# Attention and slot 0 of a fused attention and expert kernel, written out as one list of pieces with named PSUM banks

## The chip, the cores and the metric

The kernel runs on one core of one Trainium2 chip. The metric is the device time of one execution in microseconds (us); the median of several executions is compared. TensorE is called PE here, VectorE DVE, ScalarE ACT, GpSimd POOL and SyncE SP, as in the profile.

## The reference

The kernel computes an attention over four batches of 768 tokens with eight heads of 64, whose output x (3072 tokens by 512) goes straight into a layer with eight experts, of which each token takes one. Of the attention, a token sees the neighbours closer than 16 positions, and one summary of each block of 32 tokens (the maximum of the block's keys, the mean of its values):

```python
k_sum = k.reshape(B, H, nb, block, D).max(axis=3)      # block 32, nb 24
v_sum = v.reshape(B, H, nb, block, D).mean(axis=3)
mask_l = np.abs(pos[:, None] - pos[None, :]) < window  # window 16
scores_s = scale * np.einsum('bhsd,bhnd->bhsn', q, k_sum) + np.log(block)
scores_all = np.concatenate([np.where(mask_l, scale * q @ k.T, -1e9), scores_s], axis=-1)
a = softmax(scores_all)
x = a @ np.concatenate([v, v_sum], axis=2)             # then to [3072, 512]
e_idx = np.argmax(x @ w_gate, axis=1)
...
    h = np.maximum(x[mask] @ w1[e], 0.0)               # 512 -> 1024
    ye = h @ w2[e]                                     # 1024 -> 512
    out[mask] = gate_w[mask, None] * eom[mask, e, None] * ye
```

## The kernel before, in words

The attention handles 24 tiles of 128 tokens, six to a batch; tile i is numbered by batch and place (tile 18 is the first of batch 3, and its buffers are called pr30, mn30 and so on). One tile passes these pieces. PE computes scores (L333) in two PSUM banks; DVE adds the mask (L338) and takes the smallest of each row and head, mn (L345, the scores are negated); POOL subtracts it (L350, pr<-pr,mn); ACT takes the exponential (L354); PE transposes the result (pt, L365) and ACT copies it out (L221); PE multiplies by the values (pv, L376); DVE divides by the sum (L386 to L390, into xs); the rows xs are stored to DRAM (x_dr, L395); PE transposes them (L402) and forms the router's logits (L411, L419), which DVE copies out (lg, L219).

For each batch there is preparation: the loads of k and q (raw_k, raw_q, L235, on SP's queue), a reordering copy (nat_k, nat_q, L246, most of them on POOL), transposes of them on PE (ktr, qtr, L291), copies into kt and qt on ACT (L221), the block maxima on DVE (km, L305), and their spread into kt on POOL (L312). The values are loaded into vw (L257, on SP, at the start also on POOL); their block means are summed on PE (ms, L264) and copied into each block of vw, every other copy on ACT (L221) and on DVE (L219, vw<-mst).

Once a batch has its logits, `route` finds each token's expert and its place in that expert's list: small operations on DVE (L435 to L479), counts on PE (rk, tot, L456 to L461), and one indirect DMA of POOL per tile that scatters the entries into the lists (l_dr, L484). After batches 0 and 1 a first table of slots of 256 tokens (`early_slots`, `slot_table_steps`, L699 to L765, on DVE) says which expert each slot belongs to. Slot 0 reads its list (lst, L866, POOL), gathers its rows of x (xg, L881, POOL), and PE transposes them (`take_plain`, xp, L1007) and starts with the experts' products (hp, L1017), among which the last attention pieces are placed by hand. From there on the expert slots follow one another.

All engines run in the order in which this program issues their instructions (a manual schedule). Before the change, that order comes from loops: for each tile i the loop issues scores(i + 2), values and norm of an older tile, turn_p(i), and so on, and work of other kinds is booked for a tile by `later(i, work)` in dictionaries (early, todo, put, scat, rts, end, small, mid, plan, pools). The tail from tile 21 on is written by hand. PSUM has eight banks under five tags (S, PT and PV two each, TR and MS one each). A piece takes its bank from a fixed cycle:

```python
    turn = [itertools.cycle(("TR", "S", "PT", "PV", "S", "PT", "PV"))]

    def bank(shape, name):
        tag = next(turn[0])
        return ps.tile(shape, F32, name=name, tag=tag, bufs=PB[tag])
```

A bank is free for a new piece when the operation that copies its last content out is done. `route` and the table yield a few times, so several of their small steps are issued in a row.

Of the kernel before, what the change touches and what calls it, by code (L numbers as in the profile page):

```python
# [39 lines left out]
EARLY_W = 2  # L40
# [16 lines left out]


# [143 lines left out]
def attention(tc, const, sa, sb, st, ps, dr, q, k, v, id_sb, c_sb, wg_sb, x_dr, l_dr, rt, moe, table, begin, swap):  # L202
# [56 lines left out]
    def means(b, m):  # L259
# [6 lines left out]
        if m == 2:  # L266
            nc.tensor.matmul(mp[96:P], lhsT=c_sb[0:W, C_AVG + 96:C_AVG + P], rhs=VW[b % 2][:, NB - 1, :, 0:D],
                             start=False, stop=True)
            evac(MT.rearrange("p h d -> p (h d)"), mp)

    def gather_means(b):
        mg = bank([P, H * D], f"mg{b}")
        nc.tensor.matmul(mg[LW:LW + 32], lhsT=c_sb[:, C_SUM:C_SUM + 32], rhs=MT.rearrange("p h d -> p (h d)"),
                         start=True, stop=True)
        ms[b] = sa.tile([P, H, D], F32, name=f"mst{b}", tag="mst", bufs=2) if b < B - 1 else \
# [3 lines left out]
    def put_means(b, tok):  # L279
        for blk in (2 * tok, 2 * tok + 1):  # L280
            evac(VW[b % 2][LW:LW + NS, blk, :, 0:D], ms[b][LW:LW + NS], engine="av"[blk % 2])

    ms, km, mps = {}, {}, {}

    def transposed(kind, b, u, g):
        n = nat[kind, b, u]
        pt = bank([P, 2, 256], f"{kind}tr{b}{u}{g}")
# [5 lines left out]
        return pt  # L293

    def prep_k(b, u, g):
        kt = KT[b % 2]
        pt = transposed("k", b, u, g)
        if b not in km:
            km[b] = sb.tile([P, HP, NS], F32, name=f"km{b}", tag="km", bufs=2)
        at = PAD + 4 * u * KW  # L300
        src = pt.rearrange("p x (i s) -> p x i s", s=64)
        dst = kt[:, 2 * g:2 * g + 2, at:at + 4 * KW].rearrange("p x (i w) -> p x i w", w=KW)
        evac(dst[:, :, :, 0:48], src[:, :, :, 0:48])
        evac(dst[:, :, :, 48 + NS:KW], src[:, :, :, 48:64])
        nc.vector.tensor_reduce(out=km[b][:, 2 * g:2 * g + 2, 8 * u:8 * u + 8],  # L305
                                in_=pt.rearrange("p x (n s) -> p x n s", s=32), axis=AX.X, op=ALU.max)
# [7 lines left out]
    def prep_q(b, u, g):  # L314
        qt = QT[(3 * b + u) % 2]
        evac(qt[:, 2 * g:2 * g + 2, :], transposed("q", b, u, g), -SCALE)
# [6 lines left out]
    def scores(i):  # L323
# [4 lines left out]
        for hp in range(HP):  # L328
            for y in range(2):
                blk = 2 * tok + y  # L330
                for x in range(2):
                    r = slice(64 * x, 64 * x + 64)
                    nc.tensor.matmul(sp[x][64 * y:64 * y + 64, hp, 0:W], lhsT=qt[r, hp, P * tt + 64 * y:P * tt + 64 * y + 64],  # L333
                                     rhs=kt[r, hp, blk * KW:blk * KW + W], start=True, stop=True)
        pr = sb.tile([P, 2, HP, W], F32, name=f"pr{b}{tok}", tag="pr", bufs=BUFS["pr"])
# [20 lines left out]
    def turn_p(i):  # L356
        b, tok = tiles[i]
        pr = prs.pop(i)
        e = i < HELD
        pTs[i] = (sa if e else sb).tile([W, 2, HP, P], F32, name=f"pT{b}{tok}", tag="pTe" if e else "pTl",  # L360
                                        bufs=BUFS["pTe" if e else "pTl"])
        for x in range(2):
            pt = bank([W, HP, P], f"pt{b}{tok}{x}")
            for hp in range(HP):
                nc.tensor.transpose(pt[:, hp, :], pr[:, x, hp, :], id_sb)  # L365
            evac(pTs[i][:, x], pt)

    def values(i):
        b, tok = tiles[i]
        pT = pTs.pop(i)  # L370
        pvs[i] = []
        for g in range(2):
            po = bank([P, 4, D + 1], f"pv{b}{tok}{g}")
            for h in range(4 * g, 4 * g + 4):
                for y in range(2):
                    nc.tensor.matmul(po[64 * y:64 * y + 64, h % 4, :], lhsT=pT[:, h % 2, h // 2, 64 * y:64 * y + 64],  # L376
                                     rhs=VW[b % 2][:, 2 * tok + y, h, 0:D + 1], start=True, stop=True)
            pvs[i].append(po)

    def norm(i):  # L380
# [3 lines left out]
        po = pvs.pop(i)  # L384
# [7 lines left out]
    def store_x(i):  # L392
        b, tok = tiles[i]
        n0 = b * S + tok * P
        (nc.sync if i >= 17 else nc.gpsimd).dma_start(x_dr[n0:n0 + P, :], xss[i].rearrange("p h d -> p (h d)"))  # L395
# [834 lines left out]
```

## Time and profile before

| what | value |
|---|---|
| median of three runs | 535.74 us (534.83 to 537.68) |
| the profiled execution, its own time | 536.84 us |
| its span | 535.0 us |
| mean granted clock of PE in it | 0.972 |
| PE busy | 491.0 us (92%) |
| DVE, ACT, POOL busy | 355.1, 313.1, 232.8 us |

The profiled execution is 1.10 us above the median of the three runs. Its time is the span and 1.84 us around it. The attention takes the first third of the span; the expert slots take the rest, and their matmuls make most of PE's busy time. PE's busy share is highest there, and lower in the attention.

### The profile page before, as it was taken

To read this page: it belongs to the slowest core of one execution; us is meant where nothing else is said; L and a number is where in the kernel's file an instruction comes from. 1 tells how busy PE (TensorE), PEld (TensorE's weight loads), DVE (VectorE), ACT (ScalarE), POOL (GpSimd) and SP (SyncE) were. 2 spreads that over 40 slices of the span, in tenths; PEclk is the share of its full clock that TensorE was granted. 3 is DMA by queue.
4 is the path that set the end of the run, shared out by engine and by line. 5 is a ranking of instruction groups with operands and counts; after the bars stand their busy time and mean duration, and the time that the engine had idled before them with its cause. 6 is when DMAs were issued, how large, how long until landed. Compare 5 with 4: busy or idle time off the path is not lost.

```text
span 535.0 us, 12519 instructions
## 1 busy us (share of the span) xinstructions
PE 491.0 (92%) x4348; PEld 405.3 (76%) x4348; DVE 355.1 (66%) x787; ACT 313.1 (59%) x612; POOL 232.8 (44%) x261
## 2 busy tenths in 40 slices
PE   7698999998987799999999999999999989989980
PEld 6556577486666686789898998989899869879870
DVE  3748479679876237797657667665756668668672
ACT  4475677576655545464646655554655567566581
POOL 8737535646684606736433240312224315214221
PEclk9899999998997799999999999999999999999996
DMA  9998957865329328996947748484673966967771
GB/s 235 199 236 199 278 129 179 197 154 128 82 56 324 117 92 266 242 168 193 328 141 254 254 168 312 126 310 150 245 260 137 310 212 216 319 210 228 264 238 29
DMA packets 106114, 109.53 MB, mean 205 GB/s; under 512 B 43150, under 2 KB 67886, under 8 KB 106032
## 3 DMA queue, kind: packets, MB, share of 16 engines
q1 hardware_dynamic: 97216, 90.04, 57.6%
q0 software_dynamic: 8816, 18.51, 11.4%
q8 instruction: 38, 0.62, 0.5%
q14 instruction: 44, 0.36, 0.3%
HBM read 98.33 MB, written 13.59 MB: 209 GB/s over the span
## 4 chain that ended last, share of the span: by engine, by line
PE 69%; ACT 9%; DMA 7%; issue 5%; POOL 4%; DVE 4%; SPq 1%; POOLq 0%; ACTq 0%; DVEq 0%
PE yp L1128 8%; PE yp L1127 8%; PE yp L1126 8%; PE hp L950 8%; PE hp L949 8%; PE hp L948 8%; PE pt L365 3%; PE hp L1017 3%; PE yp L1031 3%; PE pv L376 3%; PE sp L333 2%; ACT pr L354 2%; DMA raw<-in_moe_w_dram 2%; PE xp L930 2%; ACT pT L221 2%
## 5 line engine op out<-in xcount | busy, mean ns | idle before, releaser
L918 DVE TENSOR_TENSOR w2l<-raw,w2h 128x512 fp32r<-128x512 f32 x120 | 79.4, 685 | 40.3 <-ACT w2h L917 38.7
L917 ACT ACTIVATE w2h<-raw 128x512 fp32r<-128x512 f32 x120 | 72.9, 628 | 54.8 <-PE yp L1128 23.7
L950 PE MATMUL hp<-xhl,w1l 128*128 128x256 f32 x352 | 99.4, 283 | 0.0
L949 PE MATMUL hp<-xhl,w1h 128*128 128x256 f32 x352 | 99.4, 283 | 0.0
L948 PE MATMUL hp<-xhl,w1h 128*128 128x256 f32 x352 | 99.4, 284 | 0.0
L881 POOL DMA_INDIRECT xg<-x_dr,lst x34 | 39.3, 1155 | 118.1 <-PE xp L930 110.6
L918 DVE TENSOR_TENSOR w1l<-raw,w1h 128x512 fp32r<-128x512 f32 x117 | 74.5, 687 | 14.8 <-ACT w1h L917 13.5
L1126 PE MATMUL yp<-w2h,hh 128*128 128x512 f32 x200 | 80.1, 400 | 0.0
L1128 PE MATMUL yp<-w2h,hl 128*128 128x512 f32 x200 | 78.7, 394 | 0.1
L1127 PE MATMUL yp<-w2l,hh 128*128 128x512 f32 x200 | 78.6, 393 | 0.0
L917 ACT ACTIVATE w1h<-raw 128x512 fp32r<-128x512 f32 x120 | 67.0, 621 | 8.4 <-DMA raw<-in_moe_w_dram 6.9
L949 PEld LDWEIGHTS hp<-xhl,w1h 128*128 128x128 f32 x352 | 67.4, 191 | 1.1 <-issue 0.2
L948 PEld LDWEIGHTS hp<-xhl,w1h 128*128 128x128 f32 x352 | 67.2, 191 | 1.2 <-issue 0.2
L950 PEld LDWEIGHTS hp<-xhl,w1l 128*128 128x128 f32 x352 | 67.4, 192 | 0.0
L951 ACT ACTIVATE hh<-hp 128x256 fp32r<-128x256 f32 x88 | 33.4, 380 | 52.0 <-PE hp L950 50.4
L350 POOL TENSOR_TENSOR pr<-pr,mn 128x960 f32<-128x960 f32 x24 | 43.1, 1797 | 46.1 <-DVE mn L345 29.1
L952 DVE SCALAR_TENSOR_TENSOR hl<-hp,hh 128x256 fp32r<-128x256 f32 x88 | 35.9, 419 | 35.6 <-ACT hh L951 35.5
L1151 POOL DMA_INDIRECT out_dram<-y,lst x27 | 30.5, 1131 | 55.7 <-DVE y L1148 28.9
L221 ACT ACTIVATE pT<-pt 120x512 f32<-120x512 f32 x48 | 26.8, 596 | 41.2 <-PE pt L365 41.0
L338 DVE TENSOR_TENSOR pr<-sp,c_sb 128x480 f32<-128x480 f32 x48 | 29.2, 649 | 29.2 <-PE sp L333 29.2
L866 POOL DMA_INDIRECT lst<-l_dr,rowib x30 | 31.5, 1051 | 31.9 <-issue 21.8
L1128 PEld LDWEIGHTS yp<-w2h,hl 128*128 128x128 f32 x200 | 37.5, 188 | 8.6 <-DVE hl L1097 0.5
(206 smaller groups left out, 876.9 us busy)
## 6 DMA issues: line engine op xcount, KB each, us to landing
raw<-in_moe_w_dram SPq DMA_DIRECT2D x240, 256.0 KB, 5.2
raw_k<-in_k_dram SPq DMA_DIRECT2D x12, 512.0 KB, 6.0
raw_q<-in_q_dram SPq DMA_DIRECT2D x12, 512.0 KB, 6.2
vw<-in_v_dram SPq DMA_DIRECT2D x44, 128.0 KB, 4.9
x_dr<-xs POOLq DMA_DIRECT2D x17, 256.0 KB, 4.0
vw<-in_v_dram SPq DMA_DIRECT2D x33, 64.0 KB, 5.1
w1l<-in_moe_w_dram SPq DMA_DIRECT2D x8, 256.0 KB, 7.9
w2l<-in_moe_w_dram SPq DMA_DIRECT2D x8, 256.0 KB, 5.7
```

What stands on the lines that cost most here:

```text
L221: nc.scalar.activation(dst, src, AF.Copy, scale=1.0 if scale is None else scale)
L350: nc.gpsimd.tensor_tensor(pr, pr, mns.pop(i).unsqueeze(2).to_broadcast([P, H, W]), ALU.subtract)
L881: nc.gpsimd.indirect_dma_start(out=self.xg[t], out_offset=None, in_=self.x_dr[0:rows, :], in_offset=bass.IndirectOffsetOnAxis(ap=self.list ...
L917: nc.scalar.activation(hi, raw, AF.Copy)
L918: (lo_by or nc.vector).tensor_tensor(lo, raw, hi.bitcast(F32), ALU.subtract)
L948: nc.tensor.matmul(hp, lhsT=w_h[:, fs], rhs=self.xh[:, c, :], start=c == 0, stop=False)
L949: nc.tensor.matmul(hp, lhsT=w_h[:, fs], rhs=self.xl[:, c, :], start=False, stop=False)
L950: nc.tensor.matmul(hp, lhsT=w_l[:, fs], rhs=self.xh[:, c, :], start=False, stop=c == NC - 1)
L952: nc.vector.scalar_tensor_tensor(hl[:, j, :], hp, 0.0, hh[:, j, :].bitcast(F32), ALU.max, ALU.subtract)
L1126: nc.tensor.matmul(y, lhsT=hh[:, j, tk], rhs=w_h, start=j == 0, stop=False)
L1127: nc.tensor.matmul(y, lhsT=hh[:, j, tk], rhs=w_l, start=False, stop=False)
L1128: nc.tensor.matmul(y, lhsT=hl[:, j, tk], rhs=w_h, start=False, stop=j == NF - 1)
```

## The change

The loops, the dictionaries, the function `later` and the hand-written tail are gone. In their place stands a string of some 895 pieces, ORDER, and a table that says which function each name calls; a piece is its name, its numbers, and after a colon the letters of the PSUM banks that it takes (S, P for PT, V for PV, T for TR, M for MS). What used to be one step is split where it has parts on several engines: a transpose and the copy that empties its bank are separate pieces, and so are scores and mask. `route` (r.b, b the batch) and the first table (ta) now yield after each single operation, so that each is a piece. The engines of the copies of means are as before, but for one copy (block 31's, of tile 15) that moves from DVE to ACT. Before and after, the same operations run, the same number of them on PE. The table of the later slots, whose steps are single now too, is advanced three steps at a time (REST) and so is ready at the same place.

```diff
+REST = 3
+ORDER = """
+lk.0 lk.1 lk.2 lq.0 lq.1 lv.0.0.s lv.1.0.s cl.1 rk.0.v pk.0.0:T kk.0.0 cl.0 mk.0.0 pk.0.1:S kk.0.1 mk.0.1
+rk.1.a pk.1.0:P lv.0.1.p kk.1.0 pk.1.1:V kk.1.1 lv.1.1.p mk.1.0 mk.1.1 rk.2.p pk.2.0:T kk.2.0 pk.2.1:S lv.2.1.p kk.2.1 mk.2.0
...
-    turn = [itertools.cycle(("TR", "S", "PT", "PV", "S", "PT", "PV"))]
+    banks_of = []
...
-        tag = next(turn[0])
+        tag = {"S": "S", "P": "PT", "V": "PV", "T": "TR", "M": "MS"}[banks_of.pop(0)]
...
-    def prep_k(b, u, g):
-        kt = KT[b % 2]
-        pt = transposed("k", b, u, g)
...
+    def keep_k(b, u, g):
+        pt = banks["k", b, u, g]
...
+    def max_k(b, u, g):
...
-    for i, (b, tok) in enumerate(tiles[:n - AHEAD]):
...
-        scores(i + AHEAD)
-        for t in at[i]:
-            values(t)
-            norm(t)
...
+    for w in ORDER.split():
+        w, _, at = w.partition(":")
+        banks_of[:] = at
+        name, *args = w.split(".")
+        work[name](*(int(x) if x.isdigit() else x for x in args))
+    return [lambda: route_to(B - 1) for _ in range(TB)]
...
-            made = made or next(rest, None)
+            for _ in range(REST):
+                made = made or next(rest, None)
```

Three places show what the list moves. At the start, POOL's order around the reordering of the third part of batch 0's keys (nat_k02) was this before:

```order
L198 DMA l_dr_75<-fill_158 128x2
L215 MEMSET vw1_170 24x8x64
L246 COPY nat_k02_235<-raw_k02_182 128x1024
L257 DMA vw0_169<-in_v_dram 32x8x64 x11
L257 DMA vw0_169<-in_v_dram 16x8x64
L350 TENSOR_TENSOR pr00_317<-pr00_317,mn00_320 128x960
```

After the change it is this:

```order
L274 MEMSET vw0_169 24x8x64
L316 DMA vw0_169<-in_v_dram 32x8x64 x4
L305 COPY nat_k02_239<-raw_k02_176 128x1024
L316 DMA vw0_169<-in_v_dram 32x8x64 x5
L316 DMA vw0_169<-in_v_dram 16x8x64
L316 DMA vw0_169<-in_v_dram 32x8x64 x2
L422 TENSOR_TENSOR pr00_317<-pr00_317,mn00_320 128x960
```

Four of the twelve loads of values that POOL issues now stand ahead of that copy; the other eight stay behind it and ahead of the first subtraction (pr00).

On DVE, the steps just ahead of the smallest of tile 18 (mn30) were these before. inc1a, inc2a and inc4a belong to the first table, ssum, eo and pair to the routing of batch 1, pr31 is the mask of tile 19:

```order
L700 TENSOR_TENSOR inc2a_2194<-inc1a_2191 128x6
L699 COPY inc4a_2197<-inc2a_2194 128x4
L700 TENSOR_TENSOR inc4a_2197<-inc2a_2194 128x4
L472 TENSOR_REDUCE ssum1_2200<-ex1_2032 128x6
L473 TENSOR_SCALAR ssum1_2200<-ssum1_2200 128x6
L474 TENSOR_SCALAR eo1_2034<-eo1_2034 128x6
L475 RECIPROCAL ssum1_2200<-ssum1_2200 128x6
L476 RECIPROCAL eo1_2034<-eo1_2034 128x6
L478 TENSOR_TENSOR pair1_2206<-ssum1_2200,eo1_2034 128x6
L479 COPY pair1_2206<-tok_156 128x6
L345 TENSOR_REDUCE mn30_2209<-pr30_2137 128x8
L338 TENSOR_TENSOR pr31_2255<-sp310_2237,c_sb_68 128x480
```

After the change:

```order
L278 COPY vw0_169<-mst2_1674 24x8x64
L628 COPY inc1a_2187<-t_early_2048 128x1
L630 TENSOR_TENSOR inc1a_2187<-t_early_2048 128x7
L560 CAST posi1_2190<-pos1_2147 128x6
L563 TENSOR_REDUCE ssum1_2192<-ex1_2027 128x6
L565 TENSOR_SCALAR ssum1_2192<-ssum1_2192 128x6
L628 COPY inc2a_2195<-inc1a_2187 128x2
L630 TENSOR_TENSOR inc2a_2195<-inc1a_2187 128x6
L417 TENSOR_REDUCE mn30_2198<-pr30_2144 128x8
L567 TENSOR_SCALAR eo1_2029<-eo1_2029 128x6
L569 RECIPROCAL ssum1_2192<-ssum1_2192 128x6
L410 TENSOR_TENSOR pr31_2234<-sp310_2216,c_sb_68 128x480
```

Before, nine steps of the table (six of them stand above the rows shown) and seven of the routing lie between the copy of means into vw and mn30. Now seven steps lie there; the others have moved behind mn30, or ahead of the mask of tile 18.

On SP's queue, around the load of the first part of batch 3's queries (raw_q30), before, where vw0 is the buffer of batch 2's values:

```order
L235 DMA raw_k30_1400<-in_k_dram 128x8x128
L235 DMA raw_q30_1506<-in_q_dram 128x8x128
L257 DMA vw0_169<-in_v_dram 64x8x64
L257 DMA vw0_169<-in_v_dram 32x8x64
L257 DMA vw0_169<-in_v_dram 64x8x64
L257 DMA vw0_169<-in_v_dram 16x8x64
L235 DMA raw_k31_1518<-in_k_dram 128x8x128
```

After the change:

```order
L294 DMA raw_k30_1391<-in_k_dram 128x8x128
L316 DMA vw0_169<-in_v_dram 32x8x64 x2
L316 DMA vw0_169<-in_v_dram 64x8x64 x2
L316 DMA vw0_169<-in_v_dram 32x8x64
L316 DMA vw0_169<-in_v_dram 16x8x64
L316 DMA vw1_170<-in_v_dram 48x8x64
L316 DMA vw1_170<-in_v_dram 64x8x64
L294 DMA raw_k31_1510<-in_k_dram 128x8x128
L294 DMA raw_q30_1550<-in_q_dram 128x8x128
L294 DMA raw_k32_1627<-in_k_dram 128x8x128
```

The last loads of batch 2's values now stand ahead of the load of raw_q30 and not behind it.

Two more moves have no rows here. On PE, the values of tile 21 (16 matmuls) stand ahead of the transposes of slot 0's gathered rows (xp) and not behind them. And of the pieces that take a PSUM bank, 240 take one that an earlier piece of the list has used; counted in pieces of the list between the step that empties a bank and the piece that takes it next, the distance is six or less for 21 of them after the change (in three the emptying is written behind the taking), and for none before.

## Rows read from the trace of the kernel before

**Rows 1.** Windows by stage: busy us of each engine (and instructions), clock, DMA share.
```profile
64.00:119.00 55.00, 51.24 (x780) 37.14 (x778) 40.02 (x105) 38.56 (x75) 28.21 (x31) 1.00 0.70 173
119.00:143.00 24.00, 21.38 (x359) 16.15 (x358) 20.52 (x63) 15.07 (x32) 14.93 (x19) 0.93 0.52 111
143.00:178.70 35.70, 27.25 (x372) 19.29 (x370) 24.66 (x65) 19.44 (x33) 25.89 (x30) 0.88 0.59 186
178.70:430.00 251.30, 251.26 (x1645) 220.55 (x1646) 161.87 (x361) 140.81 (x285) 90.76 (x93) 0.99 0.67 214
```

**Rows 2.** Timeline of PE: start us, length us, work, [idle before it <- releaser].
```profile
24.36 1.09 PE L365 MATMUL pt<-id_sb,pr 128*120 128x128 f32 x8 [2.38 <-ACT pr L354]
...
25.38 1.06 PE L264 MATMUL ms<-vw,c_sb 64*32 64x512 f32 x8
...
48.95 1.54 PE L333 MATMUL sp<-kt,qt 64*64 64x120 f32 x32 [0.99 <-POOL kt L312]
...
74.12 1.25 PE L365 MATMUL pt<-id_sb,pr 128*120 128x128 f32 x8 [0.76 <-DVE km L305]
...
103.05 1.04 PE L264 MATMUL ms<-vw,c_sb 64*32 64x512 f32 x2 [1.11 <-DMA vw<-in_v_dram]
...
114.59 1.25 PE L365 MATMUL pt<-id_sb,pr 128*120 128x128 f32 x8 [0.76 <-DVE km L305]
...
128.61 0.18 PE L456 MATMUL rk<-ohb,tri 128*128 128x48 bf16 x1 [2.25 <-DVE km L305]
...
170.76 1.15 PE L376 MATMUL pv<-vw,pT 120*64 120x65 f32 x32
...
177.81 0.48 PE L1007 MATMUL xp<-id_sb,xg 128*128 128x128 f32 x1 [2.82 <-DMA xg<-x_dr,lst]
```

**Rows 3.** Timeline of SP's DMA queue: issues around the load of raw_q30.
```profile
95.76 0.39 SPq L235 DMA_DIRECT2D raw_q<-in_q_dram  x1
96.24 2.63 SPq L257 DMA_DIRECT2D vw<-in_v_dram  x4
```

**Rows 4.** Timeline of POOL: the start, then the road to the gather xg.
```profile
10.68 1.03 POOL L246 COPY nat_k<-raw_k 128x1024 f32<-128x1024 f32 x1
...
11.66 4.26 POOL L257 DMA_DIRECT2D vw<-in_v_dram  x7
...
138.54 1.04 POOL L246 COPY nat_q<-raw_q 128x1024 f32<-128x1024 f32 x1
...
143.36 1.78 POOL L350 TENSOR_TENSOR pr<-pr,mn 128x960 f32<-128x960 f32 x1 [3.78 <-DVE mn L345]
...
156.20 0.97 POOL L484 DMA_INDIRECT l_dr<-pair,posi  x1 [0.19 <-DVE mn L345]
...
158.18 1.80 POOL L350 TENSOR_TENSOR pr<-pr,mn 128x960 f32<-128x960 f32 x1
...
165.60 1.02 POOL L866 DMA_INDIRECT lst<-l_dr,rowia  x1 [5.62 <-DMA l_dr<-pair,posi]
```

**Rows 5.** Timeline of DVE: copies of means into vw, and mn30.
```profile
44.72 0.42 DVE L219 COPY vw<-mst 24x512 f32<-24x512 f32 x1
...
123.83 1.31 DVE L219 COPY vw<-mst 24x512 f32<-24x512 f32 x1
...
138.68 1.19 DVE L219 COPY vw<-mst 24x512 f32<-24x512 f32 x1
...
142.07 1.14 DVE L345 TENSOR_REDUCE mn<-pr 128x8 f32<-128x960 f32 x1
...
158.42 1.84 DVE L219 COPY vw<-mst 24x512 f32<-24x512 f32 x1
```

**Rows 6.** Windows behind three idle times of PE (columns as in rows 1).
```profile
24.40:28.00 3.60, 3.60 (x54) 2.43 (x55) 1.95 (x3) 1.98 (x3) 3.60 (x3) 1.00 0.94 148
129.20:132.60 3.40, 3.40 (x24) 2.25 (x24) 3.16 (x12) 1.85 (x3) 3.20 (x7) 0.50 0.93 219
177.40:184.20 6.80, 5.94 (x51) 5.20 (x52) 1.70 (x6) 3.75 (x8) 4.95 (x5) 0.53 0.07 23
```

More of the change, by code (lines that the diff above doesn't have):

```diff
@@ L59, in most @@
+"""
 def most(h):
@@ L383, in norm @@
         den = st.tile([P, H], F32, name=f"den{b}{tok}", tag="den", bufs=BUFS["den"])
-        po = pvs.pop(i)
+        po = [banks.pop(("pv", i, g)) for g in range(2)]
         for g in range(2):
@@ L452, in route @@
         nc.scalar.activation(ex, d, AF.Exp)
+        yield
         eo = tmp("eo", [P, TB])
         nc.scalar.activation(eo, o1, AF.Exp, scale=-1.0)
+        yield
         rk = bank([P, TB + 1, E], f"rk{b}")
@@ L488, in route @@
             rt["scatters"].append(i.ins)
-    steps = [(b, u) for b in range(B) for u in range(3)]
     routes = {}
@@ L517, in attention @@
-    for tok in range(2, TB):
-        load_vw(0, tok, (0,))
-    for g in range(2):
-        prep_q(*steps[0], g)
-    k_sum(0, "v")
-    for u in range(3):
-        load("k", 1, u)
-    n = len(tiles)
-    live, at, held = {}, {}, []
-    for i in range(n):
-        at[i] = []
-        for _ in range(2):
-            if i > HELD and held:
-                live[held[0]] = i
-                at[i].append(held.pop(0))
-        held.append(i)
-    live[n - 1] = n
-    early, todo, put, scat, rts, end, small, mid = {}, {}, {}, {}, {}, {}, {}, {}
@@ L538, in later @@
-    def later(i, work, when=todo):
-        when.setdefault(i, []).append(work)
-    for s in range(2, len(steps)):
-        later(2 * s - 3, lambda s=s: [prep_q(*steps[s], g) for g in range(2)])
-    for b in range(1, B):
-        for tok, gs in ({2: (0, 1), 3: (2, 3, 4, 5)} if b == 1 else {0: (0, 1), 1: (2, 3), 2: (4, 5)}).items():
-            for x in gs:
-                later(TB * (b - 1) + tok, lambda b=b, x=x: prep_k(b, x // 2, x % 2))
-    for b in range(B):
-        first = live[TB * b]
-        for m in range(3):
-            later(first - (3 if b == 0 else 4) + m, lambda b=b, m=m: means(b, m), early if b == 0 and m == 2 else todo)
-        later(first - 1 - (b > 0), lambda b=b: gather_means(b), end if b else early)
@@ L552, in attention @@
-    for t in range(n):
-        first = live[t - t % TB]
-        later(max(live[t] - 2, first - 1), lambda t=t: put_means(*tiles[t]), put)
-    for i in range(AHEAD):
-        scores(i)
-        smallest(i)
-        subtract(i)
-        if i == 0:
-            reorder("q", *steps[1], "a")
-            load("q", *steps[3])
-            for g in range(2):
-                prep_q(*steps[1], g)
-            exps(0)
-    for i in range(3):
-        later(live[2 * TB - 1] + 4 + i, table, small)
-    plan = {
-        live[2 * TB - 1] + 6: [begin],
-        n - AHEAD - 1: [moe.take_plain],
-    }
@@ L633, in attention @@
-    assert not small and not plan and not pools and not scat and not early and not end
-    b = B - 1
-    def first(j, *n):
-        moe.early_first(j)
-        for x in n:
-            moe.split(1, x)
-    t = n - AHEAD
-    values(t - 1)
-    norm(t - 1)
-    turn_p(t)
-    exps(t + 1)
-    for x in put.pop(t):
-        x()
-    for x in mid.pop(t, []) + rts.pop(t, []):
-        x()
-    assert not todo.pop(t, None) and not put and not todo and not rts and not mid
-    store_x(t - 1)
-    first(0, "v", "p")
@@ L1055, in full_with @@
             if not self.slots.get(EARLY):
-                made = made or next(rest)
+                for _ in range(REST):
+                    made = made or next(rest)
                 if made:
```

395 lines of the change are left out of this document (199 added, 196 removed).

## The prediction

> **What bounds the kernel now.** I read the windows by stage first. From 178.7 us on PE has no gap: it is busy for 251.26 of 251.30 us up to 430 [rows 1]. In the three attention stages ahead of that it stands idle for 3.76, 2.62 and 8.45 us, at a clock of 1.00, 0.93 and 0.88 [rows 1]. So the expert slots cost what they cost, and the end of the kernel follows from the moment at which PE can begin them without a gap. That moment is the landing of xg, slot 0's gathered rows, for which PE waits 2.82 us until 177.81 [rows 2]. A change that only orders attention, routing and first table can move the end by what it moves that landing, and by the PE work that it takes from behind it.
>
> Next I followed xg back on POOL. The list lst is issued at 165.60, after 5.62 us of waiting for the scatters into l_dr to land; the last scatter is issued at 156.20; and the work that leads to it begins with the subtraction at 143.36, which waited 3.78 us for mn30 [rows 4]. From there to the last scatter POOL stands still nowhere for more than 0.2 us: two subtractions, two stores of x, seven scatters. So two things set xg: when DVE delivers mn30 (tile 18), which hangs on PE's and DVE's progress up to there, and then a run of POOL and DMA work of about 34 us that the change leaves as long as it is.
>
> The progress up to mn30 is that of PE with its waits. Those that matter are listed in the timeline: 0.99 us for the spread of km into kt, twice 0.76 us for km (the bank to be taken was still read by DVE), 1.11 us for a load of vw, 2.25 us for km again [rows 2].
>
> **The change, place by place.** All terms are for the profiled execution of 536.84 us; it lies 1.10 us above the median of 535.74, and I carry the sum over to the median as it stands. Nothing is removed or added, so each term is a wait that goes or comes.
>
> *The start.* Four POOL loads of vw now stand ahead of the copy nat_k02, which before began at 10.68 without a wait [rows 4]. Seven such loads took 4.26 us, 0.61 each [rows 4], so nat_k02 comes 2.43 us later, and behind it the last keys, the maxima, the first queries and the first scores. On the other side PE waited 2.38 us for the first exponential at 24.36, and the first group of block means, 1.06 us, which stood behind that wait [rows 2], now stands ahead of it and fills it. The wait of 0.99 us at 48.95 goes as well, since values of tiles 2 and 3 stand ahead of those scores now. 2.43 - 1.06 - 0.99 is +0.4 us. Bounds: +2.4, if neither cover holds, and -2.0, if the load order hides the whole delay behind other waits.
>
> *64 to 119 us.* The two waits of 0.76 us on km end, because the transposes of P after them take banks that were emptied long before; the 1.11 us on vw ends, because those loads no longer stand behind the load of raw_q30. That load was issued at 95.76 and the four loads behind it from 96.24 on, over 2.63 us [rows 3]; it can only go when POOL has emptied the buffer of raw_q, and nothing of this holds the vw loads. Together -2.6 us. Bounds: -3.8, all that PE stands idle in this stage [rows 1], and 0, if another wait takes their place.
>
> *119 to 143 us.* A copy of means that takes 1.31 us on DVE at 123.83 [rows 5] goes to ACT. DVE is the engine that PE waits for here (2.25 us, [rows 2]). But the counts rk, which ended that wait, now stand behind the values of tile 14, and these in turn wait for the last km of that batch, so 1.15 us of PE work (a group of values at 170.76, [rows 2]) that was done ahead of the wait comes behind it. -1.31 + 1.15 is -0.2 us. Bounds: -1.3 and +1.2, one of the two without the other.
>
> *The steps ahead of mn30.* Between the copy of means, which ends at 138.68 + 1.19 = 139.87, and mn30 at 142.07 lay 16 small steps in 2.20 us [rows 5]; seven are left, so 9/16 of that goes, 1.24 us. The copy itself took 1.19 us where others take 0.42 [rows 5], and it ended 0.29 us after POOL's copy nat_q of 138.54 did [rows 4]. That POOL copy now stands ahead of a scatter rather than behind it, some 2 us earlier, and so the copy of means should again take 0.42: 0.77 us. Together -2.0 us. Bounds: -2.0 and 0, if PE's scores for tile 18 come late and DVE waits instead. The steps taken out cost DVE the same time elsewhere, in its idle time ahead of masks. Of the seven scatters three instead of four are now ahead of tile 19's subtraction; their number up to the last one stays.
>
> *The wait for xg.* The values of tile 21, 1.15 us at full clock [rows 2], move from behind the transposes of xg to ahead of them, into the 2.82 us of waiting. -1.15 us; bounds 0, if xg landed when PE had just come, and -2.3, at half clock.
>
> The sum is 0.4 - 2.6 - 0.2 - 2.0 - 1.15 = -5.55 us: 531.3 us for an execution like the profiled one, 530.2 us for the median. All bounds together would be +3.6 and -11.4 us.
>
> **The rivals.**
>
> *Banks that are taken too early: slower.* The reuse of a PSUM bank within six pieces of its emptying occurs 21 times now and never before, in tiles 3 to 7, 12 to 14 and 19 to 23 above all. A wait of PE on a bank that DVE has not emptied was 0.76 us [rows 2]. At that price eight such waits (6.1 us) eat the gain, and twelve make it 9.1 - 5.55 = +3.6 us, 539.3 us. For it: DVE and ACT run one behind the other on each tile, and a piece written two places behind an emptying waits for it in full. Against it: with two banks to a tag and scores two tiles ahead, part of them will be free in time.
>
> *Steps held beside POOL: no change.* The copy of means at 158.42 took 1.84 us instead of 0.42; POOL's subtraction ran from 158.18 to 159.98, and the copy ended 0.28 us after it [rows 4, 5]. So such an operation of DVE stands still while POOL's runs. The change puts a step of that kind right behind the smallest of tiles 11, 14, 17 and 19, where that tile's subtraction begins on POOL. At 1.42 us each that is 5.7 us, which eats the sum: 535.9 us. Against it: DVE often has the first word there, since it goes on at once. The Trainium skill (SBUF — State Buffer, section Who interferes with whom) says so in general: a DVE instruction with two SBUF inputs, or in a mode that uses both ports, and a GpSimd instruction that reads SBUF lock each other out for a whole instruction, and the one issued first wins. The trace agrees for the copies, 1.84 against 0.42 us; for the small steps no row here shows it.
>
> *The scatters' landing sets the end: only the last term is left.* The wait of 5.62 us ahead of lst [rows 4] falls where the weights of slot 0 are loaded. If these loads start earlier by as much as PE does, the scatters meet them earlier too and land when they landed before. Then xg stays, and only the values moved into the wait count: 535.74 - 1.15 = 534.6 us. For it: a scatter takes up to 9 us from issue to landing here (156.20 to 165.60); against it: the scatters are issued ahead of the weights' loads in both orders.
>
> *The clock comes back too: a larger gain.* After the waits of 2.25 and 2.82 us the granted clock is 0.50 for 3.40 us and 0.53 for 6.80 us, the lower of its two levels (1.2 of 2.4 GHz) [rows 6]. Half of 3.40 and 0.47 of 6.80 are 4.9 us. If the shorter waits leave the clock up, 530.2 - 4.9 = 525.3 us. Waits of up to 1.11 us left it at 1.00 [rows 1, 2]; after the 2.38 us at 24.36 it was 1.00 too [rows 2, 6], so the wait before does not settle it. The Trainium skill (TensorE: Matmul & The Clock Gate, part 1) has an idle engine drop to half and a busy one return; the trace agrees on the two levels. By that rule a filled wait is worth more than its length.
>
> **How the numbers follow.** The forecast has 0.44, its own range is 527.5 to 533 us. The clock rival has 0.16, the landing 0.16, the held steps 0.10, the banks 0.14. A measurement of this kernel can tell about 0.5%, 2.7 us, from no change. Faster by more: the forecast, the clock, and 0.06 of the landing and the held steps, in which part of the early terms survives; 0.66. Within: the rest of these two and 0.02 of the banks; 0.22. Slower: 0.12. The range from 524.5 to 537.0 us leaves out the banks beyond their deciding point and a fifth of the clock's cases.
>
> **What the changed profile would show.** nat_k02 should begin near 13.1 us and the first scores 2 us later than before; no wait on km between 64 and 119 us, none on vw at the last group of means; the copy of means ahead of mn30 at 0.42 us with seven steps behind it; the subtraction of tile 18 about 4.4 us earlier, near 139; lst near 161; xg about as much earlier, with a wait of some 1.7 us ahead of it; and a PE without gaps behind it. I am wrong if new waits of PE on DVE or ACT appear with short bank distances, if lst still goes at 165, or if PE gets gaps behind xg, because weights or lists for the later slots then come too late.

## The result, and the profile after

The changed kernel took 528.50 us (median of four, 526.94 to 529.75) against 536.31 us of the kernel before in the same comparison (median of four): ratio 0.9854, 95% interval 0.981 to 0.9897, faster. The forecast was 530.2 us in a range of 524.5 to 537.0. The profiled execution took 527.46 us, with a span of 525.4 us; the one before had 535.0 us, so the traces differ by 9.6 us. On the two chips of the experiments the same changed kernel measured 1.0056 and 1.0055 times the kernel before, so the gain did not come again; what stands behind this is part of the experiments. Some executions of every kernel fall into a slower state, and the medians in the experiments leave them out.

The windows of the stages after, for [rows 1] (the columns are the same; the last two windows are cut at the landing of xg, which came earlier):

```profile
core 0: us, PE busy (x) PEld busy (x) DVE busy (x) ACT busy (x) POOL busy (x), PEclk, DMA share, GB/s
64.00:119.00 55.00, 51.79 (x783) 36.94 (x781) 38.98 (x102) 39.98 (x77) 28.43 (x28) 0.97 0.82 180
119.00:143.00 24.00, 22.23 (x383) 17.27 (x377) 21.53 (x66) 17.05 (x35) 18.74 (x26) 1.00 0.52 122
143.00:174.00 31.00, 26.18 (x408) 17.96 (x405) 24.37 (x74) 20.99 (x35) 25.58 (x31) 1.00 0.59 200
174.00:430.00 256.00, 255.91 (x1652) 224.27 (x1653) 167.48 (x366) 145.75 (x294) 92.02 (x94) 1.00 0.65 217
```

From 64 to 119 us PE idles for 3.21 of 55.00 us where it was 3.76, at a clock of 0.97 where it was 1.00; it idles less behind that, and from 174 us on it is busy for 255.91 of 256.00 us. The clock is 1.00 in the two stages ahead of xg, where it was 0.93 and 0.88.

PE's timeline (start, duration, operation, and in brackets the wait ahead of it and what ended it), for [rows 2]:

```profile
14.02 1.97 PE L359 MATMUL ktr<-id_sb,nat_k 128*128 128x128 f32 x8 [2.72 <-POOL nat_k L305]
...
18.15 1.97 PE L359 MATMUL qtr<-id_sb,nat_q 128*128 128x128 f32 x8 [2.16 <-DVE nat_q L305]
...
27.36 1.09 PE L432 MATMUL pt<-id_sb,pr 128*120 128x128 f32 x8 [0.71 <-ACT pr L426]
...
31.25 1.09 PE L432 MATMUL pt<-id_sb,pr 128*120 128x128 f32 x8 [1.82 <-ACT pr L426]
...
44.85 0.69 PE L447 MATMUL pv<-vw,pT 120*64 120x65 f32 x16 [0.98 <-DVE km L373]
...
77.50 1.20 PE L447 MATMUL pv<-vw,pT 120*64 120x65 f32 x32 [1.73 <-DVE km L373]
...
172.59 0.33 PE L945 MATMUL xp<-id_sb,xg 128*128 128x128 f32 x1 [0.31 <-DMA xg<-x_dr,lst]
...
174.09 0.55 PE L945 MATMUL xp<-id_sb,xg 128*128 128x128 f32 x3 [1.17 <-DMA xg<-x_dr,lst]
...
176.18 1.89 PE L955 MATMUL hp<-xhl,w1l 128*128 128x256 f32 x8
```

POOL's timeline, for [rows 4]:

```profile
10.54 2.34 POOL L316 DMA_DIRECT2D vw<-in_v_dram  x4
...
12.93 1.03 POOL L305 COPY nat_k<-raw_k 128x1024 f32<-128x1024 f32 x1
...
24.48 1.79 POOL L422 TENSOR_TENSOR pr<-pr,mn 128x960 f32<-128x960 f32 x1 [3.87 <-DVE mn L417]
...
28.36 1.79 POOL L422 TENSOR_TENSOR pr<-pr,mn 128x960 f32<-128x960 f32 x1 [2.10 <-DVE mn L417]
...
141.96 1.79 POOL L422 TENSOR_TENSOR pr<-pr,mn 128x960 f32<-128x960 f32 x1 [2.21 <-DVE eo L567]
...
154.58 0.96 POOL L581 DMA_INDIRECT l_dr<-pair,posi  x1
...
156.97 1.79 POOL L422 TENSOR_TENSOR pr<-pr,mn 128x960 f32<-128x960 f32 x1 [1.42 <-DVE mn L417]
...
160.37 1.02 POOL L805 DMA_INDIRECT lst<-l_dr,rowia  x1 [0.63 <-issue]
...
166.36 1.03 POOL L820 DMA_INDIRECT xg<-x_dr,lst  x1 [0.95 <-DMA lst<-l_dr,rowia]
```

DVE's steps around mn30, for [rows 5]:

```profile
139.31 0.67 DVE L278 COPY vw<-mst 24x512 f32<-24x512 f32 x1
...
140.59 0.16 DVE L630 TENSOR_TENSOR inc2a<-inc1a 128x6 f32<-128x6 f32 x1
...
140.67 1.15 DVE L417 TENSOR_REDUCE mn<-pr 128x8 f32<-128x960 f32 x1
```

Three lines of the trace before that the table needs, from the timelines of POOL, of SP's queue (the first loads of slot 0's weights) and of PE (its first products), and the loads' line after the change:

```profile
23.70 1.79 POOL L350 TENSOR_TENSOR pr<-pr,mn 128x960 f32<-128x960 f32 x1 [0.43 <-DVE mn L345]
...
155.84 5.42 SPq L979 DMA_DIRECT2D w1l<-in_moe_w_dram  x8
...
184.32 1.97 PE L1017 MATMUL hp<-xhl,w1l 128*128 128x256 f32 x8
```

```profile
156.34 5.46 SPq L918 DMA_DIRECT2D w1l<-in_moe_w_dram  x8
```

The subtraction L350 (now L422) comes once per tile on POOL and dates each tile in both traces; the lines above and rows 4 give some of the starts. Read so, the 9.6 us come from the places in the table (after minus before, us). The last column is the same difference for a second pair of traces, of the runs again2 (the changed kernel) and control (the order before), both on one chip of the experiments; its 1.3 us are the difference of their spans, 538.1 and 539.4. Of the forecast for the start, the 0.99 us at 48.95 lie behind tile 1, so +1.4 and -3.6 stand in the first two rows.

| from | to | change there | forecast | second pair |
|---|---|---|---|---|
| start | subtraction of tile 1 (23.70, now 28.36) | +4.66 | +1.4 | +3.65 |
| there | subtraction of tile 15 (119.21, 123.83) | -0.04 | -3.6 | +0.17 |
| there | subtraction of tile 17 (134.90, 135.79) | -3.73 | -0.2 | -3.73 |
| there | subtraction of tile 18 (143.36, 141.96) | -2.29 | -2.0 | -2.29 |
| there | lst (165.60, 160.37) | -3.83 | 0 | +0.35 |
| there | end of the last wait for xg (178.74, 174.09) | +0.58 | 0 | -1.10 |
| there | first products of slot 0 (184.32, 176.18) | -3.49 | -1.15 | -2.46 |
| there | end of the span (535.0, 525.4) | -1.46 | 0 | +4.11 |

The total is right and most of the terms are not: the start loses three times what I gave it, the stage behind it gains nothing, and what carried the result are the stage up to tile 17, the landing of the scatters and the clock behind xg. Of these three the second pair shows the first and the last again, and not the landing.

### The profile page after: what moved, and what is told of

Read it like the earlier page. It is cut to its first block, busy times and chain, and to the rows that moved or that the text cites. A ratio compares the mean times of both kernels' runs of the same rounds, so it can differ in the third digit from the quotient of the medians.

```text
span 525.4 us, 12487 instructions
## 1 busy us (share of the span) xinstructions
PE 484.8 (92%) x4348; PEld 401.7 (76%) x4348; DVE 354.6 (67%) x786; ACT 314.3 (60%) x613; POOL 232.8 (44%) x261
## 4 chain that ended last, share of the span: by engine, by line
PE 74%; DVE 8%; ACT 4%; POOL 4%; issue 3%; DMA 3%; POOLq 0%; DVEq 0%; ACTq 0%
PE yp L1072 8%; PE yp L1070 8%; PE yp L1071 8%; PE hp L889 8%; PE hp L888 8%; PE hp L887 8%; PE hp L955 3%; PE yp L969 3%; PE pv L447 3%; PE sp L400 2%; PE pt L432 2%; PE xp L869 2%; DMA raw<-in_moe_w_dram 2%; DVE pr L410 2%; PE qtr L359 2%
## 5 line engine op out<-in xcount | busy, mean ns | idle before, releaser
L820 POOL DMA_INDIRECT xg<-x_dr,lst x34 | 40.7, 1197 | 111.8 <-PE xp L869 99.6
L422 POOL TENSOR_TENSOR pr<-pr,mn 128x960 f32<-128x960 f32 x24 | 43.2, 1800 | 44.1 <-DVE mn L417 29.5
L1070 PEld LDWEIGHTS yp<-w2h,hh 128*128 128x128 f32 x200 | 37.7, 188 | 7.4
```

The source lines that it names most:

```text
L422: nc.gpsimd.tensor_tensor(pr, pr, mns.pop(i).unsqueeze(2).to_broadcast([P, H, W]), ALU.subtract)
L820: nc.gpsimd.indirect_dma_start(out=self.xg[t], out_offset=None, in_=self.x_dr[0:rows, :], in_offset=bass.IndirectOffsetOnAxis(ap=self.list ...
L1070: nc.tensor.matmul(y, lhsT=hh[:, j, tk], rhs=w_h, start=j == 0, stop=False)
```

## The experiments

Each time stands beside a ratio to the kernel before on the same chip; the runs went out in three groups of four, each on one chip. The ratio isn't the quotient of the two medians, so a difference between two kernels of a group comes out a little otherwise by ratios than by medians; where that matters both are given. The hybrids are cut from the two lists, the order before being written in the notation of the change with the banks that its cycle gave.

**The start as before, the rest changed (start54).** The first 54 pieces, up to the subtraction of tile 0, are those of the order before.

```diff
-rk.1.a pk.1.0:P lv.0.1.p kk.1.0 pk.1.1:V kk.1.1 lv.1.1.p mk.1.0 mk.1.1 rk.2.p pk.2.0:T kk.2.0
+rk.1.a pk.1.0:P kk.1.0 mk.1.0 pk.1.1:V kk.1.1 mk.1.1 rk.2.p pk.2.0:S kk.2.0 mk.2.0
...
-sc.0:SP ma.0 mi.0 su.0
+lv.0.1.p lv.1.1.p lv.2.1.p lv.3.1.p lv.4.1.p lv.5.1.p
...
+sc.0:SP ma.0 mi.0 su.0
```

> The changed list, but its first 54 pieces (up to the subtraction of tile 0) stand in the order of before: the copy nat_k02 ahead of all loads of values on POOL, the bank letters of before with it. Theory A (the new start costs some 4.5 us, which is carried on to the end because nothing ahead of xg absorbs it): the first subtraction near 21.5 us instead of 24.5, the subtraction of tile 13 some 3 to 4.5 us earlier than in the changed kernel, the time 524 to 525.5 us, a ratio to before near 0.979. Theory B (the delay is absorbed: POOL's scatters and the loads of weights set when xg lands): as the changed kernel, 528 us, ratio near 0.985.

Measured: 538.6 us, ratio 0.9980 (0.9950 to 1.0010). Its first subtraction is at 21.39 us, tile 13's at 102.62. The earlier start came, as theory A had it, and the time of theory A didn't.

**Order before up to tile 13, changed behind it (late13), and the reverse (early13).** Both are joined at the subtraction of tile 13.

```diff
 late13: pieces before, lk.0 ... su.13 | the changed list's other pieces in its order
 early13: changed pieces, lk.0 ... su.13 | the other pieces in the order before
```

> The order of before up to the subtraction of tile 13 (427 pieces), the changed order from there on. Theory A (all of the gain arises behind tile 13, and the start is a loss): faster than the changed kernel by the 4.4 us that its tile 13 lies behind, 524 us, ratio 0.978. Theory B (start and middle do not matter, the end of attention sets xg): 528 us, ratio 0.985. If the middle (64 to 119 us) gained as the prediction says, it is slower than the changed kernel by 2 to 3 us: 531 us, ratio 0.990.

> The changed order up to the subtraction of tile 13, the order of before from there on. Theory A: slower than before by the 4.4 us: 540 us, ratio 1.008. Theory B: as before, ratio 1.000. If the middle gained as the prediction says: faster than before by 2 to 3 us, ratio 0.995.

Measured: late13 539.3 us, 0.9987 (0.9955 to 1.0019), with tile 13 at 103.99; early13 544.17 us, 1.0072 (1.0041 to 1.0104), with tile 13 at 108.49, lst at 168.99 and the last transposes of xg at 183.47. The changed order up to tile 13 alone is slower, by 4.5 us at that tile.

**Changed up to tile 20, the tail as before (tail20).**

```diff
 changed pieces, lk.0 ... su.20 | the other pieces in the order before
```

> The changed order up to the subtraction of tile 20 (684 pieces), the order of before from there on; the values of tile 21 stand behind the transposes of xg again. Theory A (the scatters land 4 to 5 us earlier since none of POOL's copies stands ahead of them, and that is in the part kept): lst still near 160.5 us, xg near 172 to 174, the values again behind xg for 1.15 us and the clock low behind a wait of about 2.5 us, 3 us more: 531 to 533 us, ratio 0.992. Theory B (the gain is made behind tile 20, by what PE does in the wait for xg): 535 to 536 us, ratio 0.999.

Measured: 538.0 us, 0.9994 (0.9960 to 1.0028), profiled span 533.1 us. Its lst goes out at 160.83, near the 160.5 of theory A, and the ratio is that of theory B; what decides lies behind slot 0, as the run control shows further down.

None of the four stood where the first comparison would put it, so the next four, on another chip, began with the changed kernel itself.

**The changed kernel unaltered (again), and the start as before once more beside it (start54b).** No edit; and that of start54.

> The changed kernel unaltered, so that the edits beside it are compared on one chip. Theory A and theory B both: ratio to before 0.985, as in its own measurement. If the chip of the first four experiments is what made them slow (each of them had stretches behind 200 us in which PE, ACT and DVE all waited for nothing that the profile shows), the ratio here tells how much of the gain such a chip leaves: 0.985 on a chip like the first one, 0.99 to 1.00 on one like the second.

> The kernel start54 again, beside the changed kernel on one chip. Theory B (the delay of the start is absorbed between tile 18 and xg): the same time as the changed kernel within 1.5 us, first transposes of xg within 1 us of it. Theory A (the delay is carried to the end): 4 us faster.

Measured: again 542.51 us, 1.0056 (1.0028 to 1.0084); start54b 537.19 us, 1.0003 (0.9964 to 1.0042). So the start before makes the changed list faster on one chip, by 5.3 us by the medians and 2.9 by the ratios. In the traces the first subtraction comes 2.7 us earlier (21.62 instead of 24.34), tile 13's 6.2, and the last transposes of xg 6.3 (172.69 instead of 178.98): nothing up to xg takes a late start up. Some 1.2 us of that may be the one trace of again, since again2, the same list, has these transposes at 177.74.

The trace of again shows a part of why the ratio is not that of the first comparison. Behind slot 0 PE gets single instructions with pauses for which no semaphore is the cause ("issue"), though it had no gap there in both first traces:

```profile
223.39 0.28 PE L884 MATMUL hp<-xhl,w1h 128*128 128x256 f32 x1 [1.04 <-issue]
...
224.81 0.37 PE L885 MATMUL hp<-xhl,w1h 128*128 128x256 f32 x1 [1.14 <-issue]
...
227.64 0.37 PE L884 MATMUL hp<-xhl,w1h 128*128 128x256 f32 x1 [1.53 <-issue]
...
230.44 0.37 PE L886 MATMUL hp<-xhl,w1l 128*128 128x256 f32 x1 [1.73 <-issue]
```

**The last scatter of batch 1 later (scat).**

```diff
-... r.1 ... mi.20 su.20
+... mi.20 su.20 r.1
```

> The changed list with one piece moved: the last scatter of batch 1 stands behind the subtraction of tile 20 on POOL, so that it is issued near 158.8 us instead of 154.6, behind the start of the loads of slot 0's weights (156.3) instead of ahead of it. Theory C (the scatters land late when they meet those loads; in the kernel before the last one was issued 0.4 us behind their start and lst waited until 9.4 us after its issue, in the changed kernel it left 1.8 us ahead of them and lst did not wait): lst at 166 to 168 us, xg some 6 us later, the time 3.5 to 5 us above the changed kernel. Rival (the landing takes its 5 us anyway): lst at 164, the time 1.5 to 2.5 us above it.

Measured: 546.55 us, 1.0142 (1.0098 to 1.0186), 4.0 us above again (4.6 by the ratios). POOL's timeline:

```profile
162.19 0.98 POOL L578 DMA_INDIRECT l_dr<-pair,posi  x1
...
168.90 1.00 POOL L802 DMA_INDIRECT lst<-l_dr,rowia  x1 [4.67 <-DMA l_dr<-pair,posi]
```

The scatter goes out 5.7 us later than in again (156.53 there) and not at 158.8 as expected, since POOL stood 4.67 us for the smallest of tile 20 before the subtraction that is now ahead of it. lst goes out 5.7 us later too (163.16 there). From the scatter to lst it is 6.7 us here, all of it landing, and 6.6 in again, where POOL did the subtraction and a copy meanwhile. So the later issue accounts for the whole shift, and the run does not show that the scatter lands more slowly behind the loads of weights: neither theory was put to the test as it stood.

**The values of tile 21 behind xg (va21).**

```diff
-va.21.0:P va.21.1:P ... tk.0 ... tk.1
+tk.0 ... tk.1 va.21.0:P va.21.1:P
```

> The changed list with the values of tile 21 behind the transposes of xg, as before. Theory of the prediction: 1.15 us of PE come back behind xg, 1 to 2 us above the changed kernel. Theory D (the wait for xg, 1.15 us longer then, makes PE fall to the lower clock behind it, as in the kernel before): 4 to 5 us above it, a granted clock near 0.5 for some us behind xg.

Measured: 544.9 us, 1.0121 (1.0079 to 1.0163), 2.4 us above again. In its trace PE waits 1.49 us for xg at 177.67, where again waits 0.35. The size (3.5 us by the ratios) agrees roughly with 1.15 us of values and as much of new waiting, but the granted clock stayed at 1.00 in both from 165 to 190 us, so this run says nothing of the clock.

The last four, on the chip of the first group, were to price the start and to find what the starved stretch belongs to.

**The changed kernel unaltered, on that chip (again2).** No edit.

> The changed kernel unaltered, as the reference for the other three on this chip. If PE runs without a gap from the first xp to 250 us, as in the first profile, the ratio to the kernel before should be near 0.985; if PE has the stretch behind slot 0 (from about 222 us) in which it gets an instruction only every 0.7 us or more, near 1.000 to 1.006, as on the chip of the second comparison.

Measured: 541.33 us, 1.0055 (1.0025 to 1.0085), with the stretch.

**Only nat_k02 ahead of the loads (nat2).**

```diff
-rk.1.a pk.1.0:P lv.0.1.p kk.1.0 pk.1.1:V kk.1.1 lv.1.1.p mk.1.0 mk.1.1 rk.2.p pk.2.0:T
+rk.1.a pk.1.0:P rk.2.p lv.0.1.p kk.1.0 pk.1.1:V kk.1.1 lv.1.1.p mk.1.0 mk.1.1 pk.2.0:T
```

> The copy nat_k02 alone goes ahead of the four loads of vw; all else is the changed list. Theory L (the four loads are the price of the start): the copy begins 2.4 us earlier, near 10.5 us, the first subtraction comes at least 2 us earlier (22.4 or before instead of 24.5), tile 13's subtraction 2.5 to 4.5 us earlier, and the end comes 2 to 4.5 us earlier than that of the unaltered list. Rival (the order of the first queries and scores, or the half clock between 14 and 24 us, sets the start): the first subtraction gains under 1 us, and so does the end.

Measured: 540.02 us, 1.0032 (0.9997 to 1.0067), 1.3 us below again2 and within its interval. POOL's timeline:

```profile
10.82 1.03 POOL L302 COPY nat_k<-raw_k 128x1024 f32<-128x1024 f32 x1 [0.21 <-PE ktr L356]
...
21.43 1.80 POOL L419 TENSOR_TENSOR pr<-pr,mn 128x960 f32<-128x960 f32 x1
...
24.69 1.79 POOL L419 TENSOR_TENSOR pr<-pr,mn 128x960 f32<-128x960 f32 x1 [1.46 <-DVE mn L414]
...
29.42 1.04 POOL L302 COPY nat_q<-raw_q 128x1024 f32<-128x1024 f32 x1 [2.94 <-DMA raw_q<-in_q_dram]
...
30.42 1.79 POOL L419 TENSOR_TENSOR pr<-pr,mn 128x960 f32<-128x960 f32 x1
```

The first two subtractions come 2.9 us earlier than in again2 (24.33 and 27.54), as theory L had it, and the third doesn't (30.42, there 30.27): the next copy of queries now waits 2.94 us for its load. That load is the third of raw_q on SP's queue; eight loads of vw stand ahead of it where the order before has four, and it goes out at 19.18 us instead of 15.12. Tile 13 gains 0.93 us, less than two traces of the unaltered list differ there (107.43 and 108.68). Neither theory holds as it stood: the four loads on POOL are one price of the start, and behind it stands a second, the load of queries that comes behind more values on SP.

**The scatters spread out (thin).**

```diff
+    r["pad"] = const.tile([P, 256], F32, name="pad")
...
             nc.gpsimd.memset(rt["gap"][:, g:g + 1], 0.0)
+            if b >= 2:
+                for _ in range(3):
+                    nc.gpsimd.memset(rt["pad"], 0.0)
```

> The changed list with three small writes of POOL (256 columns each, about 0.3 us each by the rows of such writes) ahead of each scatter of batches 2 and 3, so that these twelve go out at about 2.2 us each rather than 1.27. Theory S (the run of scatters is what starves PE behind slot 0): PE's idle time between 210 and 250 us falls from some 7 us to under 3, and the end comes 4 to 9 us earlier than that of the unaltered list. Rival W (the weights' loads and PE's own place in its instructions do it): still 5 us idle or more, the end within 2 us, or later, since lst of the later slot waits for scatters that come up to 11 us later. Where the unaltered list has no such stretch on this chip, the run tells nothing but the price of later scatters.

Measured: 537.96 us, 0.9972 (0.9937 to 1.0006), 3.4 us below again2 by the medians and 4.5 by the ratios. Windows of 5 us (busy us of each engine, granted clock, DMA share, GB/s) of again2:

```profile
core 0: us, PE busy (x) PEld busy (x) DVE busy (x) ACT busy (x) POOL busy (x), PEclk, DMA share, GB/s
210.00:215.00 5.00, 5.00 (x14) 2.19 (x12) 3.67 (x13) 1.63 (x4) 4.11 (x8) 1.00 1.03 367
215.00:220.00 5.00, 5.00 (x43) 4.94 (x42) 1.56 (x3) 1.07 (x2) 4.01 (x7) 1.00 0.93 276
220.00:225.00 5.00, 1.65 (x10) 1.25 (x8) 1.53 (x10) 0.00 (x0) 4.24 (x9) 0.86 0.87 259
225.00:230.00 5.00, 1.75 (x6) 1.36 (x5) 0.00 (x0) 0.00 (x0) 2.91 (x5) 0.50 0.14 41
230.00:235.00 5.00, 4.65 (x25) 4.36 (x25) 3.60 (x23) 2.86 (x8) 0.00 (x0) 0.62 0.00 0
235.00:240.00 5.00, 5.00 (x33) 4.51 (x32) 4.83 (x17) 3.94 (x9) 0.00 (x0) 1.00 0.21 56
```

And of thin:

```profile
core 0: us, PE busy (x) PEld busy (x) DVE busy (x) ACT busy (x) POOL busy (x), PEclk, DMA share, GB/s
210.00:215.00 5.00, 5.00 (x23) 3.09 (x22) 3.64 (x10) 0.84 (x2) 4.45 (x11) 1.00 0.86 279
215.00:220.00 5.00, 5.00 (x44) 5.00 (x44) 4.08 (x20) 1.80 (x5) 4.46 (x13) 1.00 1.04 342
220.00:225.00 5.00, 5.00 (x44) 5.00 (x43) 4.62 (x25) 2.06 (x5) 4.06 (x9) 1.00 0.51 153
225.00:230.00 5.00, 5.00 (x24) 4.12 (x23) 4.86 (x17) 3.65 (x8) 4.40 (x12) 1.00 0.57 109
230.00:235.00 5.00, 5.00 (x28) 4.14 (x27) 5.00 (x10) 4.04 (x8) 4.57 (x7) 1.00 0.22 15
250.00:255.00 5.00, 4.03 (x20) 3.07 (x19) 2.83 (x5) 3.01 (x7) 3.84 (x4) 1.00 0.74 245
255.00:260.00 5.00, 0.72 (x3) 0.73 (x4) 1.09 (x3) 0.98 (x2) 3.22 (x4) 0.66 0.82 292
```

PE's 6.95 us of idle time between 210 and 250 us, and the half clock behind them, are gone. In their place the later slot's rows come late: the last scatter goes out at 240.61 us, and PE waits for xg:

```profile
259.28 0.66 PE L870 MATMUL xp<-id_sb,xg 128*128 128x128 f32 x2 [5.26 <-remote]
```

These 5.26 us of new idle time stand against the 6.95 that went, and the end gains 3.4 or 4.5 us, at the edge of the 4 that I had as the least. (The spans of the two traces differ by 4.7 us, but 1.7 of them stand already at the first products of slot 0, ahead of what the edit touches.) With the scatters spread out the stretch is gone, as theory S had it. The edit also moves them up to 13 us later, and whether the spacing or the later place helps, and by which way the scatters hold PE up, isn't shown.

**The order before in the form of the list (control).** No piece is moved against the kernel before.

> The order and the banks of the kernel before, written in the form of the list: every engine issues what it issued before the change. Ratio 1.000, within 0.4%. Theory C (the starved stretch belongs to the chip): PE stands idle for 2 us or more between 210 and 260 us here too, as it did for 2.7 us in the two hybrids that end with the order before. Rival (it belongs to the changed list): no gap there, as in the first profile of the kernel before.

Measured: 538.12 us, 0.9992 (0.9956 to 1.0027). PE's timeline:

```profile
232.78 0.28 PE L886 MATMUL hp<-xhl,w1h 128*128 128x256 f32 x1 [1.04 <-issue]
...
233.51 0.28 PE L887 MATMUL hp<-xhl,w1l 128*128 128x256 f32 x1 [0.45 <-issue]
```

PE is idle for 2.40 us between 230 and 235 us, for which the first profile of the kernel before has none. So in these runs the stretch is there in either order; whether it is the chip that makes the difference to the first comparison isn't shown. The form of the list costs nothing.

How long the stretch is goes with the order behind tile 20. PE's idle time from 210 to 250 us is 2.40, 2.60 and 2.71 us in the three runs that end in the order before (control, early13, tail20), 6.70 to 7.55 us in the eight that end in the changed order with its scatters close together, and none in thin. tail20 and again2 have the changed order up to tile 20, stand level at the first products of slot 0 (179.23 and 179.01) and end at 533.1 and 538.1 us. The window of tail20 with all of its idle time:

```profile
225.00:230.00 5.00, 2.29 (x18) 2.13 (x17) 2.84 (x18) 0.90 (x2) 3.11 (x5) 1.00 0.92 248
```

So the tail of the changed list costs 5 us in these two traces against the tail before (3.3 us by the medians, 541.33 and 538.0), though the first comparison had no such stretch.

## Why the prediction was right, and where it was not

**That the total was right is luck in part.** The start missed by 3.3 us and the stage behind it by 3.6; the stage up to tile 17 and the landing gained 3.5 and 3.8 us that no term had. Even lst came near the 161 of the forecast by such a balance (160.37): tile 18 came at 141.96 and not near 139, and the landing made up for it.

**What bounds the kernel** held. The first products of slot 0 moved by 8.14 of the 9.6 us, and in the first comparison PE had no gap behind them. In the second pair they moved by 5.41 us, and the stretch behind them took most of it back.

**The start** is the step that was most mis-sized: +4.66 up to tile 1 where +1.4 stood, beyond the upper bound of +2.4, and +3.65 in the second pair. nat_k02 began at 12.93 as forecast (13.1). But PE's wait for it, 2.72 us where it was 0.58, is followed by the lower clock: eight transposes take 1.97 us where [rows 2] has eight at 1.09 (the granted clock is 1.00 from 8 to 11.3 us, 0.93 in the wait and 0.51 from 14 to 24 us; before it was 0.83 in those last ten), which I had not counted. Nor had I followed SP's queue: the four more loads of values ahead of raw_q, which nat2 uncovered. The covers that I set against the delay exist (the wait for the first exponential fell from 2.38 to 0.71 us, that for the spread of km is gone) but a wait of 1.82 us for the next exponential and, behind tile 1, one of 0.98 us for km came in. start54b shows that this cost was carried to the end.

**64 to 119 us.** From tile 1 to tile 15 the change gave -0.04 instead of -3.6 us (the -2.6 of this stage, and the -0.99). The waits of 0.76 us on km are gone, and a single one of 1.73 us on km stands at 77.50: that was the lower bound of the gain, "another wait takes their place". It is the rival of banks taken too early in one place, at twice the price that I gave it (values of tile 6 take the bank of a transpose of keys five pieces behind its emptying); nothing shows it in eight. The rival of the held steps is not seen either: the small steps right behind the smallest of tiles 11, 14, 17 and 19 take 0.06 to 0.22 us each, and of DVE's 23 copies of means the median is 0.42 us, with one at 1.36 and one at 1.88. Whether the gain is there behind an early start is open: start54 passes tile 13 at 102.62, and the order before at 103.99 (late13), 103.89 (control) and 102.37 (the first profile).

**119 to 143 us** gave -3.73 instead of -0.2. The wait of 2.25 us ahead of the counts, and with it the half clock behind it, are gone; the longest wait in this stage is 0.72 us and the clock 1.00. I had set 1.15 us of values against the copy that moved to ACT, and no wait took that up. The second pair has the same -3.73. That this comes from the copy alone was argued and not tried; steps of the routing moved in this stage as well.

**The steps ahead of mn30** gave -2.29 for -2.0. The copy of means took 0.67 us (forecast 0.42), and the seven steps between it and mn30 took 0.69. The second pair has the same -2.29.

**The scatters' landing** was a rival for the wrong sign. lst gained 3.83 us more than tile 18 did: the wait of 5.62 us is 0.63 us, not for the scatters. Here the step that failed is that the run of POOL and DMA work from mn30 to xg stays as long as it is, and the prediction's reason, scatters ahead of the weights' loads in both orders, is not so: before, the last scatter went out at 156.20, 0.36 us behind the first of these loads (155.84); after, at 154.58, 1.76 us ahead of it (156.34). But the gain did not come again (+0.35 in the second pair), and that the loads make the difference isn't shown. Where the scatter's landing is what lst waits for, it is 9.40 us from the last scatter to lst in the first profile before and 6.71 in scat, both behind the first load, and 6.07 in control and 6.94 in early13, both ahead of it. The order before alone so gives 9.40 and 6.07 us, and most of the 3.83 lies within that. Why that one landing took 9.40 us stays open.

**The wait for xg and the clock.** The values of tile 21 (32 matmuls, and not 16 as in the section on the change) moved into the wait, and the clock rival came true at this place: 1.00 instead of 0.53 behind xg. Together -3.49 us, where the transposes of xg, the values, eight transposes of another tile and its small products had run at half clock, the values alone for 2.00 us; the second pair has -2.46. The Trainium skill (TensorE: Matmul & The Clock Gate, part 1) has an idle engine drop to the lower level; here waits of 0.87 and 1.17 us at 170.53 and 174.09 left the clock at 1.00, and the one of 2.72 us at the start did not.

**Why the experiments show no gain.** From the last group of the transposes of xg to the end of the span it is 350.5 us in the first trace after (525.4 - 174.91) and 360.4 in again2 (538.1 - 177.74): 9.9 us more. For the order before it is 356.3 (535.0 - 178.74) in the first trace and 359.7 in the control (539.4 - 179.69): 3.45 more. So behind xg the chip of these two runs takes 6.4 us more from the changed list than from the order before, most of the 7.8 us of the first comparison. 4.55 of the 6.4 are the idle time of the stretch (6.95 - 2.40). Some 1.4 more are an estimate for the low clock: PE's busy time times the missing share of the clock is 2.9 us in again2 (220 to 235 us) and 1.5 in control (230 to 240). Up to xg it takes another 1.9 us (2.83 against 0.95). Together that is 8.3 of the 10.9 us that lie between the ratios 0.9854 and 1.0055; the last 2.6 us I can't place, as the control's profiled execution lies 3.1 us above its own median. "PE gets gaps behind xg" stood among the things that would make me wrong, but for late weights or lists; here it goes with a run of scatters. With either the late start or the close scatters taken away the changed list is level with the order before on these chips (1.0003, 0.9972).

A version with the start of the order before and the scatters spread less widely was not tried. start54b and thin each take their share off (5.3 and 3.4 us by the medians against the unaltered list on the same chip), and whether they add up is open.

## What to carry to other kernels

A wait early in a chain costs its length and the clock behind it, and the next load in the queue may stand right behind it: follow each queue that feeds the delayed engine, one step further than the wait that goes. Issue a scatter whose landing is waited for early: moved behind one subtraction that stood waiting, it went out 5.7 us later and cost 4.0. Don't issue many of them back to back while PE has no slack, and look at what comes late when they are spread out. A gain of one or two per cent is worth a second chip before one relies on it, and a sum of terms a second pair of traces: here six of eight places came again within 2 us, and the two that didn't decided the result.

## What the runs showed of the hardware that was not expected

On two chips PE ran for some 10 us with pauses of 0.3 to 1.7 us between single matmuls and no wait that the profile shows, during and just behind a run of scatters that POOL issued every 1.27 us. In again2 the DMA share was 0.87 to 1.03 from 210 to 225 us, and the pauses went on at 0.14 from 225 to 230; at 2.2 us and more between scatters they were absent. The Trainium skill (Runtime: NRT & Kernel Launch, section Instruction fetch mechanics) describes that each engine's instructions are brought in by DMA. That this supply ran late would fit pauses without a semaphore, but no run here shows it, and the traces speak against it: no instruction packet lands from 225 to 235 us in again2 or from 226 to 240 in again, while PE pauses for 1.73 us at 229.21 and at 230.44, so what it ran there would have been brought in before.
